# A planned attention and feed-forward block: first loads on two queues, another count of filler products, mode switches in the planner, priorities by a table

## The chip, the cores and the metric

The kernel runs on one core of a Trainium2 chip. The core has five engines that work side by side, each on its own queue of instructions: TensorE (PE in the profile; PEld are its weight loads), VectorE (DVE), ScalarE (ACT), GpSimd (POOL) and SyncE (SP), which here only issues transfers. ScalarE can issue transfers too. The metric is device microseconds of one execution; the figure for a kernel is the median of several runs.

## The reference

The input `x` has 2048 tokens of 448 values in bf16. It is normalized once, and both branches use the result:

```
xn = layernorm(x)
q, k, v = split(xn @ wqkv)               # 16 heads of 28
logits[s, w] = q[s] . k[s - 2 w] / sqrt(28)    # w = 0..7, masked where s - 2 w < 0
A = (softmax(logits) @ v[s - 2 w]) @ wo  # each token looks at 8 tokens, two apart
B = gelu(xn @ w1 + b1) @ w2 + b2         # 448 -> 1792 -> 448
out = x + A * silu(B)
```

## The kernel before

The even tokens stand in one half of the token axis and the odd ones in the other, so that "two apart" becomes "next to one another". There are 16 tiles of 128 tokens (`NT`), four chunks of 512 (`CH`), and 18 attention blocks (`BLK`) of 112 or 128 queries, each with the 128 keys before and at them.

A product of depth 448 is three products of depth 128 and a tail of depth 64. Tails of two results are put side by side in the two halves of the array (64-row mode): `batch` (L391 to L420) makes two "closed" jobs (their three full products first, then the tail) and two "opened" ones (tail first), with all tails of a batch in one task. Scores (`attn`, L541) use depth 28 and run four at a time in 32-row mode.

The stages of work, by function:

- `stats`, `rstds`, `norm`: statistics of a tile on VectorE (L341, L342), the square root on ScalarE (L351), `rstd` and the normalized tile `xn` on VectorE (L354, L369, L371). Tiles 0 to 7 are transposed by TensorE (L381) and copied to `xnT` by VectorE or ScalarE (L376 to L381); tiles 8 to 15 by a transposing DMA that SP issues.
- `qk`: query and key products of four heads each (L430, L433), in pieces of 256 tokens for the first chunk and of 512 after it. `vproj`: value products of a block (L450, L453). For these the columns of `wqkv` for queries and keys are loaded into `wraw` and spread to `wqk`, 28 columns padded to 32, by ScalarE or VectorE (L324 to L333).
- `ff1`: the first feed-forward product (L472, L475) and gelu on ScalarE with the bias `b1` (L479). `b1` is loaded as rows, transposed by TensorE (L628) and copied by VectorE (L632).
- `ff2`: the second feed-forward product (L498), bias, tanh and the gate `g` (L514, L520, L524).
- `attn`: scores, exp on ScalarE (L547), the mask on VectorE (L555), the product with the values (L562, PV below), normalization (L569, L574), then a transposing DMA into `oT`.
- `final`: the product with `wo` (L589), gate (L594), residual (L599), store (L603).

No order is written by hand. Each piece of work becomes a `_Task` with an engine (or two that could do it), a cost in us, the tasks that it depends on, buffers that it takes and gives, and a priority. `_Plan.run` (L73 to L123) lists the tasks that are ready, finds the one that could start first, and of all that could start on its engine within 0.12 us (`SLACK`) takes the one with the highest priority. `emit` then issues the instructions in the order of the planned starts; every engine carries out its queue in that order, so a wait of one instruction holds up all behind it. A task that may run on ScalarE or VectorE is put where it would end first. Priorities are numbers in the code: for the first chunk's work 95 to 99, for chunk stages `p` in `project` (L654), `100 - c` for attention (L675), `85 - c` and `60 - 4 * c` for the feed-forward products (L679, L691).

At the beginning nothing can be multiplied, so up to 40 filler products on a tile of zeros are planned on TensorE with the lowest priority, each with a cost of 0.26 us (L272 to L276). A batch of tails carries 0.12 us more in its cost for the array's change of mode (`SWITCH`, L255).

Loads (`dma`, L290) are planned as an issue on SP or ACT of 0.45 us and a transfer of so many KB at 310 KB per us, with 1.7 us until it has landed. All but the second tile of `x` are issued by SP: `x` tile 0, `wv`, `wraw` and its tail `wraw3`, `x` tiles 2 and 3, `b1`, then the rest.

Of the kernel before, what the change touches and what calls it, by code (L numbers as in the profile page):

```python
# [14 lines left out]
SLACK = 0.12  # L15
TABLE = 1.28


# [9 lines left out]
class _Task:  # L28
    __slots__ = ("eng", "cost", "deps", "fn", "prio", "take", "give", "slots",
                 "start", "end", "on", "ndep", "users", "tail", "seq", "table", "limit")  # L30


class _Plan:
# [6 lines left out]

    def add(self, eng, cost, fn, deps=(), prio=0, take=(), give=(), tail=0.0, table=(), limit=None):
# [4 lines left out]
        t.fn, t.prio, t.give, t.tail, t.table, t.limit = fn, prio, give, tail, table, limit  # L46
        t.take = {}
# [12 lines left out]

    def _at(self, t, e, free):
        at = free.get(e, 0.0)
        for p, n in t.take.items():
            if len(p.free) < n or p.fifo and p.fifo[0] is not t:
                return None
            at = max(at, sorted(p.free)[n - 1][0] + HOP)
        if t.table and self.table not in t.table:
            at += TABLE
        for d in t.deps:
            at = max(at, d.end - d.tail + 0.02 if d.on == e else d.end + HOP)  # L70
        return at

    def run(self):  # L73
# [4 lines left out]
        free = {}  # L78
        self.table = None
        ready = [t for t in self.tasks if not t.ndep]  # L80
        order = []
        while ready:
            cand = []
            for t in ready:
                ways = []
                for e, c in zip(t.eng, t.cost):
                    at = self._at(t, e, free)
                    if at is not None:
                        ways.append((at + (c if len(t.eng) > 1 else 0.0), at, e, c))
                if ways:  # L90
                    _, at, e, c = min(ways)
                    cand.append((at, t, e, c))
            if not cand:
                raise RuntimeError("the plan is stuck: " + str([(t.seq, t.eng, t.fn.__qualname__) for t in ready[:20]]))
            first = min(cand, key=lambda k: k[0])
            near = [k for k in cand if k[2] == first[2] and k[0] <= first[0] + SLACK]
            at, t, e, c = min(near, key=lambda k: (-k[1].prio, k[0], k[1].seq))
            if t.limit is not None and at > t.limit:
                t.fn, c = None, 0.0
            t.on, t.start = e, at  # L100
            if t.table and self.table not in t.table:
# [42 lines left out]
def kernel(  # L144
# [13 lines left out]
    P = 128  # L158
# [90 lines left out]
    def act(n):  # L249
        return 0.19 + n / 1200.0  # L250

    def dve(n, r=1):
        return 0.15 + n / (960.0 * r)

    SWITCH = 0.12  # L255

# [14 lines left out]
    t_warm = plan.add("DVE", 0.3, memset("vector", warm[:], 0.0), [t_on], prio=100)  # L271
    for _ in range(40):  # L272
        def fn(k):
            nc.tensor.matmul(buf(p_b, k)[:], warm[:, :P], warm[:], start=True, stop=True)  # L274
        t_warm = plan.add("PE", 0.26, fn, [t_warm], -1, take=(p_b,), limit=12.0)
        t_warm.give = ((p_b, t_warm, 0),)  # L276
# [10 lines left out]
    t_vw = [plan.add("DVE", 0.08, memset("vector", v[:, :, DH:DH + 1], 1.0), [t_on], prio=96) for v in p_v.bufs]  # L287
    t_E = [plan.add("DVE", 0.08, memset("vector", e[:, :, NQ:], 0.0), [t_on], prio=95) for e in p_E.bufs]

    def dma(eng, dst, src, kb, prio, deps=()):  # L290
        def fn(_):
            (nc.sync if eng == "SP" else nc.scalar).dma_start(dst, src)
        a = plan.add(eng, 0.45, fn, [t_on] + list(deps), prio)
        return plan.add("DMA", kb / 310.0, lambda _: None, [a], prio, tail=1.7)

# [14 lines left out]
    def ktiles(ap):  # L310
# [78 lines left out]
    def batch(close, opened, prio):  # L389
# [9 lines left out]
        def f2(k):  # L399
            todo = [[(j, i) for i, j in enumerate(every) if j.half == h] for h in range(2)]  # L400
            while todo[0] or todo[1]:
                for h in range(2):
                    if todo[h]:
# [3 lines left out]
                        else:  # L407
                            j.tail(buf(p_b, k, i - len(close)), True, False)
        tt = plan.add("PE", pairs * pe(every[0].n) + SWITCH, f2, f + [d for j in opened for d in j.deps] + [d for j in every for d in j.late],
                      prio + 0.3, take=sum(((p_b,) + j.into for j in opened), ()), give=((p_tok, f[0], 0),), tail=0.15)  # L410
        for i, j in enumerate(close):
# [54 lines left out]
    def ff1(c, mt, half, prio, gate):  # L466
# [10 lines left out]
        def evac(a, own, i):  # L477
            def fn(k):
                nc.scalar.activation(buf(p_h, own, i)[:], buf(p_b, own, i)[:], ACT.Gelu_apprx_tanh,  # L479
                                     bias=b1[:, mt:mt + 1])  # L480
            t_h[(c, mt)] = plan.add("ACT", act(CH) + 0.05, fn, [a, t_b1] + gate, prio + 3,
                                    give=((p_b, own, i),), table=("gelu",))
# [48 lines left out]
    def attn(b, prio, gate, early):  # L531
# [5 lines left out]
        def f1(k):  # L537
            for g in range(G):
                for hl in range(4):
                    r = slice(32 * hl, 32 * hl + 32)  # L540
                    nc.tensor.matmul(buf(p_b, k, hl)[:, g * nq:(g + 1) * nq], kT[g][r, k0:k0 + P],  # L541
                                     qT[g][r, q0:q0 + nq], start=True, stop=True)
        a = plan.add("PE", 0.34, f1, deps + early, prio, take=(p_b,) * 4, tail=0.15)
        pv, exps = [], []
        for hl in range(4):
# [18 lines left out]
            pv.append(plan.add("PE", 0.105, f4, [w, t_v[b]] + pv[-1:], prio + 3, take=() if hl else (p_b,),  # L564
                               give=((p_E, e, 0),) + ((v_at[b],) if hl == 3 else ()), tail=0.15))
# [5 lines left out]
        r = plan.add("DVE", 0.18, f5, [pv[-1]], prio + 4, take=(p_rd,))  # L571

# [35 lines left out]
    for t in range(TPC):  # L608
# [10 lines left out]
    t_b2 = dma("SP", b2[:], B_b2.rearrange("(o d) -> o d", o=1).to_broadcast((P, D)), 112, 81)  # L619
    t_wo = [dma("SP", wo[:, 0:3, :], ktiles(A_wo[0:KF, :]), 336, 80),  # L620
             dma("SP", wo[:64, 3, :], A_wo[KF:D, :], 56, 79)]
# [15 lines left out]
    for m, w, n, lo, hi in masks:  # L637
# [29 lines left out]
    project(0)  # L667
    t_os = [plan.add("POOL", 0.6, memset("gpsimd", o[:], 0.0), [t_xT[3]]) for o in p_os.bufs]
    t_wo.append(plan.add("POOL", 0.4, memset("gpsimd", wo[64:, 3, :], 0.0), [t_xT[3]]))
# [58 lines left out]
```

## Time and profile before

| | us |
|---|---|
| median of 6 runs | 172.37 |
| lowest and highest | 171.96, 172.57 |
| the profiled execution | 172.63 |
| its span, first to last instruction | 170.6 |
| TensorE busy in the span | 163.5 |
| VectorE, ScalarE busy | 109.4, 107.8 |

The profile is of one execution. In a row of the timeline the first number is the start in us after the first instruction, the second the length; "x4" is the number of instructions; brackets give the idle time of the engine before it and what ended that. "L472" is line 472 of the kernel. A busy TensorE is not one at its peak, as products overlap; the distance from start to start says how fast they go. In a row of windows, each engine's busy time in the stretch is followed by its number of instructions. The four digits rows of the page cut the span in 40 equal slices.

### The profile page before, as it was taken

The numbers are of one execution on the slowest core, as the hardware profiler recorded it, in microseconds if no ns is written. First come the engines' busy times: TensorE is split into PE (matmuls) and PEld (weight loads), VectorE is DVE, ScalarE is ACT, GpSimd is POOL, SyncE is SP. The second block draws the span as 40 slices with busy tenths as digits, with TensorE's granted clock in tenths as the row PEclk, the third lists the DMA queues.
The fourth block names the chain that finished last, engine by engine and source line by source line (L and its number), as shares of the span: only waits on it lengthen the run. The fifth ranks groups of instructions, "written<-read, shape, count | busy, mean of one in ns | idle before, by whom it ended". The sixth has DMA issues, their size and how long they took to land.

```text
span 170.6 us, 3510 instructions
## 1 busy us (share of the span) xinstructions
PE 163.5 (96%) x1372; PEld 78.9 (46%) x1372; DVE 109.4 (64%) x298; ACT 107.8 (63%) x197; POOL 5.0 (3%) x18
## 2 busy tenths in 40 slices
PE   7999988999999999999999999999999999999990
PEld 2455543434555544444334565434465533455540
DVE  5689887219898988896004789601689951375663
ACT  3175339968785097878889584799964599611120
POOL 7300000000000000000000000000000000000000
PEclk9999999999999999999999999999999999999999
DMA  5999980001444221211100021300012320001001
GB/s 152 253 347 270 335 295 8 0 4 30 93 99 87 54 58 27 58 29 27 27 4 0 0 61 27 81 2 4 27 26 60 81 58 0 0 27 56 27 27 54
DMA packets 21740, 12.26 MB, mean 72 GB/s; under 512 B 13724, under 2 KB 21212, under 8 KB 21724
## 3 DMA queue, kind: packets, MB, share of 16 engines
q1 hardware_dynamic: 21580, 11.93, 26.0%
q8 instruction: 10, 0.16, 0.4%
q10 hardware_dynamic: 144, 0.11, 0.2%
q14 instruction: 6, 0.05, 0.1%
HBM read 7.06 MB, written 1.84 MB: 52 GB/s over the span
## 4 chain that ended last, share of the span: by engine, by line
PE 91%; DVE 5%; ACT 1%; issue 1%; DVEq 0%; ACTq 0%
PE bank L498 25%; PE bank L472 20%; PE bank L430 12%; PE bank L589 7%; PE bank L450 6%; PE bank L562 4%; PE bank L274 4%; PE bank L475 4%; PE bank L541 3%; PE bank L433 2%; PE bank L453 1%; DVE st L341 1%; PE bank L381 1%; DVE xn L369 1%; ACT L479 1%
## 5 line engine op out<-in xcount | busy, mean ns | idle before, releaser
L498 PE MATMUL bank<-w,h 128*128 128x448 bf16 x224 | 46.4, 352 | 0.0
L547 ACT ACTIVATE E<-bank 128x448 bf16<-128x448 f32 (+1 forms) x72 | 33.7, 556 | 14.5 <-PE bank L541 14.5
L472 PE MATMUL bank<-xnT,w 128*128 128x512 bf16 x168 | 39.3, 380 | 0.0
L479 ACT ACTIVATE h<-bank,b 128x512 bf16<-128x512 f32 x56 | 34.4, 692 | 2.9 <-PE bank L475 2.8
L498 PEld LDWEIGHTS <-h 128*128 128x128 bf16 x224 | 20.9, 97 | 18.5
L472 PEld LDWEIGHTS <-w 128*128 128x128 bf16 x168 | 14.9, 97 | 20.5 <-issue 5.1
L430 PE MATMUL bank<-xnT,wqk 128*128 128x512 bf16 (+1 forms) x120 | 24.3, 337 | 0.0
L555 DVE TENSOR_TENSOR E<-E,m_gen 128x448 bf16<-128x448 bf16 x64 | 22.0, 384 | 2.1 <-ACT E L547 2.0
L520 ACT ACTIVATE t<-y 128x448 f32<-128x448 f32 x16 | 9.4, 588 | 21.1 <-DVE y L514 21.1
L562 PEld LDWEIGHTS <-E 128*128 128x128 bf16 x288 | 12.7, 96 | 9.7 <-DVE E L555 2.0
L514 DVE TENSOR_TENSOR y<-bank,b 128x448 f32<-128x448 f32 x16 | 9.8, 621 | 10.8 <-PE bank L498 10.8
L524 DVE SCALAR_TENSOR_TENSOR g<-t,y 128x448 bf16<-128x448 f32 x16 | 9.9, 619 | 9.3 <-ACT t L520 9.3
L589 PE MATMUL bank<-wo,oT 128*128 128x448 bf16 x64 | 14.5, 352 | 0.3 <-DVE y L514 0.2
L261 DVE CAST kT<-bank 128x256 bf16<-128x256 f32 (+1 forms) x9 | 4.8, 534 | 15.1 <-PE bank L430 10.6
L562 PE MATMUL bank<-v,E 128*128 128x29 bf16 x288 | 14.4, 176 | 0.0
L430 PEld LDWEIGHTS <-wqk 128*128 128x128 bf16 x120 | 10.3, 97 | 8.6 <-issue 1.9
L594 DVE SCALAR_TENSOR_TENSOR sg<-bank,g 128x448 bf16<-128x448 f32 x16 | 10.0, 622 | 4.3 <-PE bank L589 3.5
L450 PE MATMUL bank<-wv,xnT 128*128 128x448 bf16 x54 | 12.6, 353 | 0.0
L574 DVE TENSOR_TENSOR os<-bank,rd 112x448 bf16<-112x448 f32 (+1 forms) x18 | 11.2, 625 | 1.0
L341 DVE BATCH_NORM_STATS2 st<-x_sb 128x6 f32<-128x448 bf16 x16 | 9.7, 604 | 1.1 <-DMA x_sb<-in_A_x_dram 1.1
L259 ACT CAST qT<-bank 128x256 bf16<-128x256 f32 (+1 forms) x13 | 6.1, 471 | 4.4 <-PE bank L433 3.0
L274 PE MATMUL bank<-warm 128*128 128x512 bf16 x19 | 7.2, 546 | 1.3 <-DVE warm L266 1.3
(52 smaller groups left out, 122.4 us busy)
## 6 DMA issues: line engine op xcount, KB each, us to landing
out_dram<-o SPq DMA_DIRECT2D x16, 112.0 KB, 1.7
w<-in_B_w_dram SPq DMA_DIRECT2D x1, 1568.0 KB, 13.6
x_sb<-in_A_x_dram SPq DMA_DIRECT2D x3, 448.0 KB, 9.1
w<-in_B_w_dram SPq DMA_DIRECT2D x1, 1344.0 KB, 10.0
wraw<-in_A_wqkv_dram SPq DMA_DIRECT2D x1, 672.0 KB, 6.4
w<-in_B_w_dram SPq DMA_DIRECT2D x2, 224.0 KB, 8.5
x_sb<-in_A_x_dram SPq DMA_DIRECT2D x3, 112.0 KB, 4.8
wv<-in_A_wqkv_dram SPq DMA_DIRECT2D x1, 336.0 KB
```

The source lines that it names most:

```text
L274: nc.tensor.matmul(buf(p_b, k)[:], warm[:, :P], warm[:], start=True, stop=True)
L341: nc.vector.bn_stats(out=s[:], in_=x_sb[:, t, :])
L430: nc.tensor.matmul(ps[:, :n], wqk[:, kt, hs, :], xnT[:, kt, cs], start=start, stop=stop)
L450: nc.tensor.matmul(ps[:, :D], xnT[:, kt, k0:k0 + P], wv[:, kt, :], start=start, stop=stop)
L472: nc.tensor.matmul(ps[:], w1[:, kt, ms], xnT[:, kt, cs], start=start, stop=stop)
L479: nc.scalar.activation(buf(p_h, own, i)[:], buf(p_b, own, i)[:], ACT.Gelu_apprx_tanh, bias=b1[:, mt:mt + 1])
L498: nc.tensor.matmul(ps[:, :D], buf(*h_at[(c, mt)])[:, j * P:(j + 1) * P], w2[:, mt, :], start=(mt == 0), stop=(mt == NMT - 1))
L547: nc.scalar.activation(buf(p_E, k)[:, :, :nq], buf(p_b, a, hl)[:, :4 * nq].rearrange("p (g q) -> p g q", g=4), ACT.Exp, scale=SCALE)
L555: nc.vector.tensor_tensor(out=E[:, :, :nq], in0=E[:, :, :nq], in1=m[:, :, :nq], op=ALU.mult)
L562: nc.tensor.matmul(ps[:, h, :DH + 1], buf(p_E, e)[:, g, :], buf(*v_at[b])[:, h, :DH + 1], start=True, stop=True)
L574: nc.vector.tensor_tensor(out=buf(p_os, k)[:nq, :D].rearrange("p (h c) -> p h c", h=H), in0=buf(p_b, po)[:nq, :].rearrange("p (h c) -> p h ...
L589: nc.tensor.matmul(ps[:, :D], oT[:, kt, t * P:(t + 1) * P], wo[:, kt, :], start=(kt == 0), stop=(kt == KT - 1))
```

## The change

Six things change, and the new order follows from all of them together.

1. *Loads.* The third k-tile of `wv` and of `wraw`, and one half of each of their tails, are issued by ACT instead of SP. The planner counts a transfer at 340 instead of 310 KB per us. Each spread of `wraw` to `wqk` depends on its own part of the load. The later tiles of `x` come after them.
2. *Fillers.* The first ten are planned at 0.43 us, the others at 0.22.
3. *Modes.* A task has a `mode` (128, 64 or 32). A TensorE task in another mode than the one before it is planned 0.095 us later, and while the array is in a tiled mode, tiled tasks get 30 more priority.
4. *Costs.* Those of ScalarE operations, gelu, the scores, PV and the reciprocal are other numbers.
5. *Priorities* of stages come from the table `PRIO`.
6. *Memsets* of `E`, of `os` (now only its last 64 columns) and of a part of `wo` go to GpSimd at the beginning.

```diff
+SWITCH = 0.095
+TILED = 30
...
+        if e == "PE" and t.mode != self.mode:
+            at = max(at, free.get(e, 0.0) + SWITCH)
         return at
...
-            at, t, e, c = min(near, key=lambda k: (-k[1].prio, k[0], k[1].seq))
+            tiled = first[2] == "PE" and self.mode != 128
+            at, t, e, c = min(near, key=lambda k: (-k[1].prio - (TILED if tiled and k[1].mode != 128 else 0), k[0], k[1].seq))
...
     def act(n):
-        return 0.19 + n / 1200.0
+        return 0.15 + n / 1130.0
...
-    SWITCH = 0.12
...
-    for _ in range(40):
+    for i in range(40):
...
-        t_warm = plan.add("PE", 0.26, fn, [t_warm], -1, take=(p_b,), limit=12.0)
+        t_warm = plan.add("PE", 0.43 if i < 10 else 0.22, fn, [t_warm], -1, take=(p_b,), limit=12.0)
...
-    t_E = [plan.add("DVE", 0.08, memset("vector", e[:, :, NQ:], 0.0), [t_on], prio=95) for e in p_E.bufs]
+    t_os = [plan.add("POOL", 0.1, memset("gpsimd", o[:, D:], 0.0), [t_on], prio=94) for o in p_os.bufs]
+    t_wo = [plan.add("POOL", 0.45, memset("gpsimd", wo[64:, 3, :], 0.0), [t_on], prio=93)]
+    t_E = [plan.add("POOL", 0.1, memset("gpsimd", e[:, :, NQ:], 0.0), [t_on], prio=95) for e in p_E.bufs]
...
-        return plan.add("DMA", kb / 310.0, lambda _: None, [a], prio, tail=1.7)
+        return plan.add("DMA", kb / 340.0, lambda _: None, [a], prio, tail=1.7)
...
-    t_wv = [dma("SP", wv[:, 0:3, :], ktiles(A_wqkv[0:KF, 2 * D:]), 336, 98)]
-    t_wv += [dma("SP", wv[64 * i:64 * i + 64, 3, :], A_wqkv[KF:D, 2 * D:], 56, 98) for i in range(2)]
-    t_raw = dma("SP", wraw[:], ktiles(A_wqkv[0:KF, 0:2 * D]), 672, 97)
-    t_raw3 = [dma("SP", wraw3[64 * i:64 * i + 64, :], A_wqkv[KF:D, i * D:(i + 1) * D], 56, 96)
+    t_wv = [dma("SP", wv[:, 0:2, :], ktiles(A_wqkv[0:2 * P, 2 * D:]), 224, 98),
+            dma("ACT", wv[:, 2:3, :], ktiles(A_wqkv[2 * P:KF, 2 * D:]), 112, 98)]
+    t_wv += [dma(("SP", "ACT")[i], wv[64 * i:64 * i + 64, 3, :], A_wqkv[KF:D, 2 * D:], 56, 97) for i in range(2)]
+    t_raw = [dma("SP", wraw[:, 0:2, :], ktiles(A_wqkv[0:2 * P, 0:2 * D]), 448, 96)] * 2
+    t_raw += [dma("ACT", wraw[:, 2:3, :], ktiles(A_wqkv[2 * P:KF, 0:2 * D]), 224, 96)]
+    t_raw3 = [dma(("SP", "ACT")[i], wraw3[64 * i:64 * i + 64, :], A_wqkv[KF:D, i * D:(i + 1) * D], 56, 95)
               for i in range(2)]
     for t in range(2, TPC):
-        load_x(t, 1, 96, "SP")
+        load_x(t, 1, 94, "SP")
...
-        t_wqk.append(plan.add(("ACT", "DVE"), (0.94, 0.39), fn, [t_raw] + t_wz, 96))
+        t_wqk.append(plan.add(("ACT", "DVE"), (0.94, 0.39), fn, [t_raw[kt]] + t_wz, 96))
...
-        tt = plan.add("PE", pairs * pe(every[0].n) + SWITCH, f2, ...
+        tt = plan.add("PE", pairs * pe(every[0].n), f2, ...
+                      mode=64)
...
-        a = plan.add("PE", 0.34, f1, deps + early, prio, take=(p_b,) * 4, tail=0.15)
+        a = plan.add("PE", 0.15, f1, deps + early, prio, take=(p_b,) * 4, tail=0.15, mode=32)
...
+    PRIO = {"project": (88.5, 80.5, 64.5, 82.5),
+            "attn": (518, 478.5, 466, 469.5),
+            "ff1": (81, 86, 47, 55),
+            "ff2": (77, 62.5, 2.5, 29.5),
+            "final": (32.5, 106.5, 13, 13.5, 16, 30, 30, 21)}
...
-        p = (80, 79, 62, 58)[c]
+        p = PRIO["project"][c]
...
-                exps += attn(b, 100 - c, gate, gels)
+                exps += attn(b, PRIO["attn"][c], gate, gels)
...
-            p = 85 - c
+            p = PRIO["ff1"][c]
...
-                ff2(t, 60 - 4 * c)
+                ff2(t, PRIO["ff2"][c])
     for t in range(NT):
-        final(t, 62 - t if t < NT - 2 else 40)
+        final(t, PRIO["final"][t // 2])
```

More of the change, by code (lines that the diff above doesn't have):

```diff
@@ L29 @@
     __slots__ = ("eng", "cost", "deps", "fn", "prio", "take", "give", "slots",
-                 "start", "end", "on", "ndep", "users", "tail", "seq", "table", "limit")
+                 "start", "end", "on", "ndep", "users", "tail", "seq", "table", "limit", "mode")
 class _Plan:
@@ L39, in __init__, with add @@
         self.tasks = []
-    def add(self, eng, cost, fn, deps=(), prio=0, take=(), give=(), tail=0.0, table=(), limit=None):
+    def add(self, eng, cost, fn, deps=(), prio=0, take=(), give=(), tail=0.0, table=(), limit=None,
+            mode=128):
         t = _Task()
@@ L46, in add @@
         t.fn, t.prio, t.give, t.tail, t.table, t.limit = fn, prio, give, tail, table, limit
+        t.mode = mode
         t.take = {}
@@ L79, in run @@
         self.table = None
+        self.mode = 128
         ready = [t for t in self.tasks if not t.ndep]
@@ L100, in run @@
             t.on, t.start = e, at
+            if e == "PE" and t.fn is not None:
+                self.mode = t.mode
             if t.table and self.table not in t.table:
@@ L408, in f2 @@
                             j.tail(buf(p_b, k, i - len(close)), True, False)
-        tt = plan.add("PE", pairs * pe(every[0].n) + SWITCH, f2, f + [d for j in opened for d in j.deps] + [d for j in every for d in j.late],
-                      prio + 0.3, take=sum(((p_b,) + j.into for j in opened), ()), give=((p_tok, f[0], 0),), tail=0.15)
+        tt = plan.add("PE", pairs * pe(every[0].n), f2, f + [d for j in opened for d in j.deps] + [d for j in every for d in j.late],
+                      prio + 0.3, take=sum(((p_b,) + j.into for j in opened), ()), give=((p_tok, f[0], 0),), tail=0.15,
+                      mode=64)
         for i, j in enumerate(close):
@@ L480, in fn @@
                                      bias=b1[:, mt:mt + 1])
-            t_h[(c, mt)] = plan.add("ACT", act(CH) + 0.05, fn, [a, t_b1] + gate, prio + 3,
+            t_h[(c, mt)] = plan.add("ACT", 0.69, fn, [a, t_b1] + gate, prio + 3,
                                     give=((p_b, own, i),), table=("gelu",))
@@ L563, in f4 @@
                                      start=True, stop=True)
-            pv.append(plan.add("PE", 0.105, f4, [w, t_v[b]] + pv[-1:], prio + 3, take=() if hl else (p_b,),
+            pv.append(plan.add("PE", 0.12, f4, [w, t_v[b]] + pv[-1:], prio + 3, take=() if hl else (p_b,),
                                give=((p_E, e, 0),) + ((v_at[b],) if hl == 3 else ()), tail=0.15))
@@ L570, in f5 @@
                                  buf(p_b, po)[:nq, :].rearrange("p (h c) -> p h c", h=H)[:, :, DH])
-        r = plan.add("DVE", 0.18, f5, [pv[-1]], prio + 4, take=(p_rd,))
+        r = plan.add("DVE", 0.25, f5, [pv[-1]], prio + 4, take=(p_rd,))
         def f6(k):
@@ L619 @@
     t_b2 = dma("SP", b2[:], B_b2.rearrange("(o d) -> o d", o=1).to_broadcast((P, D)), 112, 81)
-    t_wo = [dma("SP", wo[:, 0:3, :], ktiles(A_wo[0:KF, :]), 336, 80),
+    t_wo += [dma("SP", wo[:, 0:3, :], ktiles(A_wo[0:KF, :]), 336, 80),
              dma("SP", wo[:64, 3, :], A_wo[KF:D, :], 56, 79)]
@@ L667 @@
     project(0)
-    t_os = [plan.add("POOL", 0.6, memset("gpsimd", o[:], 0.0), [t_xT[3]]) for o in p_os.bufs]
-    t_wo.append(plan.add("POOL", 0.4, memset("gpsimd", wo[64:, 3, :], 0.0), [t_xT[3]]))
     project(1)
```

## The prediction

> **What bounds the kernel now.** I read the page first (busy shares, slices), then the chain that ended last, then the windows of each stage, and last the two stretches of the timeline where the chain leaves TensorE.
>
> ```profile
> PE 163.5 (96%) x1372; PEld 78.9 (46%) x1372; DVE 109.4 (64%) x298; ACT 107.8 (63%) x197; POOL 5.0 (3%) x18
> PE   7999988999999999999999999999999999999990
> DMA  5999980001444221211100021300012320001001
> PE 91%; DVE 5%; ACT 1%; issue 1%; DVEq 0%; ACTq 0%
> ```
>
> TensorE is busy for 96% of the span and 91% of the chain. Its work is fixed, so only three things can move the end: when useful products begin, holes in the stream, and the price of changing the array's mode. The windows tell where holes are (columns: stretch, its length, busy time of PE, PEld, DVE, ACT, POOL, clock, DMA share, GB/s).
>
> ```profile
> 8.61:26.50 17.89, 16.60 (x130) 9.16 (x129) 15.11 (x50) 9.30 (x21) 0.00 (x0) 1.00 0.96 298
> 33.30:78.70 45.40, 45.39 (x482) 22.06 (x481) 36.27 (x95) 32.81 (x66) 0.00 (x0) 1.00 0.25 53
> 90.00:135.00 45.00, 44.70 (x479) 23.01 (x478) 29.36 (x74) 33.45 (x62) 0.00 (x0) 1.00 0.13 31
> 146.50:165.60 19.10, 19.10 (x103) 9.88 (x102) 11.51 (x21) 3.60 (x8) 0.00 (x0) 1.00 0.09 30
> ```
>
> After 26.5 us there is 0.01 + 0.30 us of idle TensorE left. So nothing after the first feed-forward stage has more than 0.3 us to give. The hole is before 26.5 us, and the timeline shows it (start, length, instruction; in brackets the idle time before it and what ended it):
>
> ```profile
> 6.35 0.15 PEld L274 LDWEIGHTS <-warm 128*128 128x128 bf16 x1 [0.28 <-issue]
> 9.40 0.94 ACT L259 COPY wqk<-wraw 128x896 bf16<-128x896 bf16 x1 [4.05 <-DMA wraw<-in_A_wqkv_dram]
> 9.45 0.74 PE L450 MATMUL bank<-wv,xnT 128*128 128x448 bf16 x3
> 10.03 0.98 PE L430 MATMUL bank<-xnT,wqk 128*128 128x256 bf16 x6
> 24.12 1.28 ACT L479 ACT_TABLE_LOAD   x1 [4.42 <-DVE b L632]
> 24.84 0.38 PE L381 MATMUL bank<-ident,xn 128*128 128x128 bf16 x4 [0.36 <-DVE xnT L261]
> 26.16 0.38 PE L381 MATMUL bank<-ident,xn 128*128 128x128 bf16 x4 [0.93 <-ACT h L479]
> ```
>
> Two things. The bias b1 reaches ScalarE only at 24.1 (its copy L632 stands behind statistics on VectorE), so the gelu table and the first gelu are late, banks stay full, and the transposes L381 stand still. From one start to the next a transpose takes 0.056 us; the group of eight at 23.88 should be followed at 24.33 and is at 24.84, the next at 25.06 and is at 26.16: 0.5 + 1.1 = **1.6 us of hole**. And the first query/key product starts at 10.03, 0.66 us after wraw landed (ACT was released at 9.40). The value products fill TensorE up to 10.03.
>
> **Mode switches and priorities.** Scores and 64-row tails put the array in another mode. From row starts, a 448-column product follows another after 0.189 us and a score group follows one after 0.285: about 0.095 us for each switch. I counted switches in the issue order of both built programs: 89 before, 89 after, with the same split by kind. So the new price and the bonus for staying in a tiled mode change the order but save 0 x 0.095 = **0 us**. Useful products are equal in number too (1353), summing to 152.6 us from the first query/key product to the end in both orders. New costs of gelu, exp and copies only change the order as well. So the priorities can win only holes: 0.3 us after 33 us. I count -0.1, with bounds -0.3 and +1.5. For the upper bound I compared ScalarE's work between the exps of successive blocks with TensorE's work between their scores. It exceeds it in three places (17.8 against 16.3, 4.5 against 4.2, 2.7 against 2.4 us), by 2.1 us in all. At the largest the next block has 2.3 us of value and 2.65 us of feed-forward products ahead of its PV products, so most of it is covered.
>
> **The b1 transpose** moves from after the query/key products to before the first value tails. Its copy on VectorE now stands after the statistics of tile 7, by my sum at about 18 us, before the first gelu. ScalarE then loads its gelu table while TensorE makes the first tiles, and tiles 4 to 7 are transposed before the stage. The 1.6 us hole goes: **-1.6**. What is late next in that stage is VectorE: from the landing of wraw to the fourth xn of the second chunk it has three weight casts (0.39, 0.39, 0.27), six statistics (0.60 + 0.18 each), six xn (0.40 + 0.20), two xnT (0.42), two q copies (0.41) and small ones, about 11.7 us, while TensorE has 9.7 us of products from its first query/key product to the stage. If wraw lands at 8.8 both end at about 21: no new hole, but no slack either. w1 landed 10.0 us after an issue at 6.86, at 16.9, and is not in the way.
>
> **The loads.** SP keeps x0, two k-tiles of wv, half of the rest, two k-tiles of wraw, half of wraw3; ACT gets x1 (as before), one k-tile of wv (112 KB), 56 KB, one k-tile of wraw (224 KB), 56 KB. That is four more issues on ACT's queue, 0.4 to 0.6 us each by SP's rows, and the fifth waits for x1 (3.24 us: a DMA semaphore is reused). ACT's first table load thus moves from 1.22 to about 3.9 and ends at 5.2; its first sqrt goes from 4.32 to 5.2. It was due at 4.3, but VectorE was busy with tile 1 until 5.0, so xn0 is about 0.4 us later. Eleven fillers at 0.427 us end at 1.26 + 4.7 = 5.96, about when xn0 is ready; before, seventeen ran to 7.57. So the transposes start a microsecond earlier and the fillers' cut is worth 1.1 us by itself, but only up to the weights.
>
> When does wraw land? In the trace 672 KB took 6.4 us from an issue at 2.98. The new SP part is issued at 2.36; by that row it lands at 2.36 + 6.4 = 8.8. The rule against this is in the Trainium skill, "DMA: Bandwidth & Descriptors", section "Issuing engines are not separate DMA queues": transfers of any issuing engine run on the same 16 DMA engines and interleave, and a second issuer saves only issue time. By the rule the SP part ends after 1400 KB instead of 1344 have passed: 9.37 + 56 KB at some 330 GB/s, about 9.5. The row for it: the DMA share from 2.5 to 4.0 us is already 1.03 at 311 GB/s. But from 4.0 to 5.5 it falls to 113 GB/s, so a microsecond of bandwidth is lost that a second stream may or may not fill. Bounds 7.6 (no dip at all) to 9.8; I take **8.8**.
>
> Now what I think matters most. ACT's order after is: sqrt, sqrt, **cast of wqk (waits for wraw), copy of xnT for tile 1**, value copies. Before, VectorE made that copy at 8.4, ahead of the weights. The second value product needs xnT of tile 1, and TensorE issues it before all query/key products. So their start is: landing 8.8, cast 0.94, copy 0.59 (as ACT's 512-wide copy of kT), tail 0.19 and switch 0.10, three products 0.57, hops 0.1: 8.8 + 2.5 = **11.3 us** against 10.03: **+1.3**. By the skill's rule it would be 12.0, +2.0. Behind that copy on ACT wait both value copies and the next sqrt; VectorE's rstd of tile 2 waits for that, with slack, since x2 lands only at about 10. The b1 load, behind wraw3 in SP's queue, is waited for by TensorE ahead of the value tails; by its place it lands 0.3 to 0.6 us after wraw, under the cast and copy (1.5 us). It would cost only if it landed later than 10.3.
>
> Memsets of E, os and a row of wo go to or forward on GpSimd: 13 small ones of 0.1 to 0.2 us, done by about 5.5; the first exp comes after 30 us. VectorE loses 0.35 us of memsets at 2.0, in a stretch where it waits for x anyway. Nothing.
>
> **Sum**, on the profiled execution (172.63 us; span 170.6, 2.0 around it): +1.3 - 1.6 - 0.1 = -0.4, a span of 170.2 and a time of 172.2. The profiled execution is 0.26 above the median of the runs, 172.37, so the forecast is **171.9**.
>
> **Rivals.**
> (a) *The dip does not return*: wraw lands at 7.6 to 8.2, the start costs 0 to +0.6, total about -1.3: 171.0. For it: 14 of 16 engines had finished wraw by 8.3, and only two held it to 9.37. Against: those are waits of single packets (1.2 us each) that two queues do not remove.
> (b) *The cast in front of the copy costs more than the hole gives*: ACT holds xnT of tile 1 until wraw has landed and been cast. At a landing of 9.8 the query/key products start at 12.3 and the feed-forward stage at 22, +2.3 - 1.6 = +0.7: 173.0, slower. It decides from a landing of about 9.5 on (+2.0 - 1.6 - 0.1 = +0.3). For it: the skill's rule above gives just that.
> (c) *New holes in the attention stages*, 1 us or more, where ScalarE's work exceeds TensorE's: 173.0. Against: before ran such stages with 0.3 us lost.
> (d) *The array goes cold*. TensorE stands still from about 8.2 to 10.4 with only a filler and small products. Granted clock reads 1.00 throughout, but the fillers' spacing (their weight loads above stand 0.43 us apart up to 6.35) went to 0.216 us only at 6.7, after 5.4 us of work. The skill, "TensorE: Matmul & The Clock Gate", Part 1, says that about 3.4 us of idleness halve the clock again. The trace had 1.6 us of hole with 0.216 us spacing after it, so the row says no cost; if it happened, 3.4 us of query/key work at half speed would cost up to 1.7: 173.6.
> (e) *The change does nothing*: start and hole cancel within 0.3.
>
> **How the numbers follow.** My sum 171.9 (own range 171.4 to 172.4): 0.40, of which 0.24 lies over 0.2% below the median (0.34 us, about what a measurement can tell), 0.14 within, 0.02 above. (a) 0.22, faster. (b) 0.20, slower. (c) 0.10 and (d) 0.06, slower. (e) alone 0.02. Faster 0.46, same 0.16, slower 0.38. The range takes in (a) to a landing of 7.6 less a little, 170.6, and (b), (c) and most of (d): 173.9.
>
> **What would show it.** First query/key product at 11.3, its wait ended by ACT's xnT copy; that copy right behind the wqk cast; b1 copied before 19 us; no idle TensorE between transposes before the first gelu; 0.2 to 0.4 us of idle TensorE after 33 us. A start before 10.5, or holes over 1 us after 33 us, would make the forecast wrong.

## The result

The changed kernel takes 170.44 us (median of 18 runs, 169.76 to 172.06), the kernel before 172.33 (37 runs beside them). The ratio is **0.9905**, with a 95% interval of 0.9884 to 0.9927: about 1.6 us faster. The forecast was 171.9, with a range of 170.6 to 173.9; applied to the 172.37 that the forecast started from, the ratio gives 170.7, at the lower end of the range. The profiled execution of the changed kernel took 171.72 us, its span is 169.1. That is 0.9 us less than the profiled execution of before, but 1.6 us less in span: 2.7 us of the changed one lie outside the span and 2.0 of the one before. (Over the 18 runs of the changed kernel the median is 1.9 outside and a span of 168.4.) So the account below is made of spans.

From the page of the changed kernel: busy times and shares of the chain.

```profile
PE 161.7 (96%) x1367; PEld 78.4 (46%) x1367; DVE 105.7 (62%) x281; ACT 112.6 (67%) x206; POOL 3.8 (2%) x26
PE 91%; DMA 5%; DVE 1%; issue 0%; ACTq 0%; DVEq 0%
```

The shares hardly differ from before; but VectorE's 5% of the chain are down to 1%, and DMA, by the load of `b1r` at the start, now has 5%. The windows of the changed kernel, with the stretch between the start and the first query/key product cut out:

```profile
8.61:11.29 2.68, 1.64 (x8) 0.68 (x9) 2.27 (x7) 2.15 (x4) 0.00 (x0) 1.00 0.88 220
11.29:26.50 15.21, 15.21 (x124) 8.69 (x123) 13.74 (x47) 11.65 (x26) 0.00 (x0) 1.00 1.00 312
33.30:78.70 45.40, 45.40 (x485) 21.82 (x484) 34.95 (x90) 35.86 (x68) 0.00 (x0) 1.00 0.25 50
90.00:135.00 45.00, 45.00 (x431) 23.01 (x430) 29.76 (x71) 31.38 (x59) 0.00 (x0) 1.00 0.15 38
```

By these rows all idle time ahead of the last product now lies before 11.29: from there TensorE is busy in the whole of each stretch. (How far such rows can be trusted is a question of its own, below.) The timeline of the changed kernel, where the forecast placed its numbers:

```profile
8.94 0.94 ACT L267 COPY wqk<-wraw 128x896 bf16<-128x896 bf16 x1 [3.18 <-DMA wraw<-in_A_wqkv_dram]
...
9.65 0.18 PE L641 MATMUL bank<-ident,b1r 14*128 14x14 bf16 x1 [1.39 <-DMA b1r<-in_B_b_dram]
...
9.78 0.58 ACT L267 COPY xnT<-bank 128x512 bf16<-128x512 bf16 x1
...
11.29 0.82 PE L443 MATMUL bank<-xnT,wqk 128*128 128x256 bf16 x6
...
17.38 0.14 DVE L645 CAST b<-bank 128x14 f32<-128x14 bf16 x1
...
20.23 1.06 PE L393 MATMUL bank<-ident,xn 128*128 128x128 bf16 x16
...
21.13 1.46 PE L485 MATMUL bank<-xnT,w 128*128 128x512 bf16 x6
...
21.97 1.28 ACT L492 ACT_TABLE_LOAD   x1
23.27 2.42 ACT L492 ACTIVATE h<-bank,b 128x512 bf16<-128x512 f32 x4
```

ScalarE casts at 8.94, copies xnT of tile 1 behind that, and the first query/key product starts at 11.29 (10.03 before). The sixteen transposes of tiles 4 to 7 stand in one row ahead of the feed-forward stage, without a bracket (before, they stood within it from 23.88 to 26.5, with two waits), and the first gelu runs at 23.27 instead of 25.42.

Three starts make the account, in us of the profiled executions:

| | before | changed | difference |
|---|---|---|---|
| first query/key product | 10.03 | 11.29 | +1.26 |
| from it to the last product | 155.95 | 152.97 | -2.98 |
| last product to the end of the span | 4.67 | 4.80 | +0.13 |
| span | 170.64 | 169.06 | -1.58 |

By the forecast's sum the useful products between add up to 152.6 us at their own spacing. So before lost 3.3 us after its first query/key product and the changed kernel loses 0.4. Where the difference of 2.98 lies can be read from start to start, each distance less the usual one between two such products:

| place in before | us |
|---|---|
| two waits between transposes, from 24.27 and from 25.01 | 0.52 + 1.09 |
| second query/key product, waits for a cast of `wqk` (from 10.15) | 0.13 |
| b1 transpose with its change of mode (19.23); in the changed kernel it stands ahead of the first query/key product | 0.2 |
| two tails one behind the other instead of side by side (26.47) | 0.22 |
| later: from 68.44, 122.31, 132.11 and 132.35 | 0.17 + 0.36 + 0.12 + 0.24 |

That is 3.1 us. The changed kernel has no such hole; 0.1 comes back in smaller delays. After 33 us it is 0.9. Two of the later holes stand in the chain of before:

```profile
122.02 0.64 DVE y L514
...
122.70 0.92 PE bank L589 x4
...
132.02 0.54 ACT E L547
...
132.61 0.92 PE bank L589 x4
```

The chain leaves TensorE for VectorE's y and for ScalarE's E, and comes back to the products with `wo`. In the changed kernel neither step is there: its second feed-forward products begin at 34.1 instead of 41.0 and its `wo` products at 64.9 instead of 54.5, so other work stands at that place. That the new order removes these waits is read from the two traces; which of the new priorities does it was not tried apart.

### The profile page after: what moved, and what is told of

Read it like the earlier page. It is cut to its first block, busy times and chain, and to the rows that moved or that the text cites. A ratio compares the mean times of both kernels' runs of the same rounds, so it can differ in the third digit from the quotient of the medians.

```text
span 169.1 us, 3502 instructions
## 1 busy us (share of the span) xinstructions
PE 161.7 (96%) x1367; PEld 78.4 (46%) x1367; DVE 105.7 (62%) x281; ACT 112.6 (67%) x206; POOL 3.8 (2%) x26
## 4 chain that ended last, share of the span: by engine, by line
PE 91%; DMA 5%; DVE 1%; issue 0%; ACTq 0%; DVEq 0%
PE bank L511 25%; PE bank L485 22%; PE bank L443 13%; PE bank L602 7%; PE bank L463 6%; PE bank L575 5%; PE bank L488 4%; PE bank L554 3%; DMA b1r<-in_B_b_dram 3%; PE bank L446 3%; DMA wv<-in_A_wqkv_dram 2%; PE bank L466 2%; PE bank L393 1%; DVE sg L607 1%; DVE o L612 0%
## 5 line engine op out<-in xcount | busy, mean ns | idle before, releaser
L568 DVE TENSOR_TENSOR E<-E,m_gen 128x448 bf16<-128x448 bf16 x64 | 22.9, 386 | 2.5 <-ACT E L560 1.9
L267 ACT CAST qT<-bank 128x512 bf16<-128x512 f32 (+1 forms) x15 | 7.5, 501 | 4.7 <-PE bank L446 3.7
L269 DVE CAST kT<-bank 128x512 bf16<-128x512 f32 (+1 forms) x6 | 3.9, 645 | 10.8 <-PE bank L443 10.6
L267 ACT CAST v<-bank 128x448 bf16<-128x448 f32 x14 | 7.4, 535 | 4.6 <-PE bank L466 2.6
```

The costliest lines, as they stand in the source:

```text
L267: nc.scalar.copy(o, i)
L568: nc.vector.tensor_tensor(out=E[:, :, :nq], in0=E[:, :, :nq], in1=m[:, :, :nq], op=ALU.mult)
```

## The experiments

Times are medians; ratios are against the kernel before, run on the same chip, with 95% intervals. "Release" is the start of ScalarE's wqk cast, that is, the landing of SP's part of wraw. In most runs tasks were moved in the finished plan, by

```diff
     plan.run()
+    def move(t, *behind):
+        plan.order.remove(t)
+        plan.order.insert(max(plan.order.index(b) for b in behind) + 1, t)
```

**The bias copied early, in the kernel before** (only the 0.14 us copy of b1 moves, right behind its transpose).

```diff
+    move(t_b1, t_b1T)
```

> The kernel before with one instruction moved: the copy of b1 on VectorE (L632) stands right behind its transpose instead of behind the statistics of tiles 8 to 10. Theory (the late bias is the cause of the hole before 26.5 us): the gelu table is loaded at about 19.7 instead of 24.1, the transposes of tiles 4 to 7 find free banks, the hole of 1.6 us goes and nothing else moves: 170.8, first query/key product still at 10.0. Rival (the hole is a shortage of banks or of VectorE that only moving the transposes ahead of the stage removes): under 0.5 us gained.

171.37 us, ratio 0.9958 [0.9935, 0.9981]; 170.8 was expected. The timeline of this run:

```profile
19.52 0.17 DVE L633 CAST b<-bank 128x14 f32<-128x14 bf16 x1 [0.37 <-PE bank L628]
...
24.93 0.61 PE L381 MATMUL bank<-ident,xn 128*128 128x128 bf16 x8 [0.36 <-DVE xnT L261]
```

b1 is there at 19.7 and the first gelu runs at 21.24. Of the two holes between transposes, the one of 1.09 us is gone; the one of 0.52 stays, and it waits for VectorE's copy of the tile before, as the bracket says. The stretch from the first query/key product to the last is 155.00 us, 0.95 less. So the late bias was 1.1 of the 1.6 us and not all of it.

**The bias copied late, in the changed kernel.** b1 is copied to a spare tile (`b1x`) as now, and from there to b1 only behind the statistics of tile 10.

```diff
-        nc.vector.tensor_copy(b1[:], buf(p_b, a)[:].bitcast(BF16)[:, :NMT])
+        nc.vector.tensor_copy(b1x[:], buf(p_b, a)[:].bitcast(BF16)[:, :NMT])
...
+    st10 = t_st[10].fn
+    def late(k):
+        st10(k)
+        nc.vector.tensor_copy(b1[:], b1x[:])
+    t_st[10].fn = late
```

> The changed kernel with b1 held back: VectorE copies it to a spare tile at 17.4 as now, and from there to its place only behind the statistics of tile 10, at about 24, as in the kernel before; the order of all else is the changed one. Theory (the late bias costs only because transposes stand in the feed-forward stage and wait for its banks; here they stand ahead of it): gelu starts 2 us later, eight banks and the two feed-forward products behind the stage cover it, 0 to +0.3 us. Rival (a late bias costs 1.6 us wherever the transposes stand): +1.6, 172.2.

170.87 us, ratio 0.9933 [0.9910, 0.9957]. Its timeline:

```profile
20.80 1.46 PE L486 MATMUL bank<-xnT,w 128*128 128x512 bf16 x6
...
23.39 0.14 DVE L719 COPY b<-b1x 128x14 f32<-128x14 f32 x1
...
23.61 1.28 ACT L493 ACT_TABLE_LOAD   x1 [1.99 <-DVE b L719]
24.90 2.42 ACT L493 ACTIVATE h<-bank,b 128x512 bf16<-128x512 f32 x4
```

The gelu comes 4.1 us after the stage's first product (2.1 in the changed kernel), the table load waits for b1 as it did before, and TensorE shows no hole: 152.94 us from first query/key to last product against 152.97. The median is 0.4 us above the changed kernel's, which these intervals don't tell apart. With the transposes ahead of the stage, the late bias costs TensorE nothing. In this order it is their place that counts, and the early bias is not needed for it. (The opposite run, the kernel before with only its transposes moved ahead of the stage, was not made.)

**The xnT copy on VectorE** (tile 1's copy goes back to VectorE, ahead of the weights).

```diff
+    t_xT[1].on = "DVE"
+    move(t_xT[1], t_xT[0], t_xT[1].deps[0])
```

> The changed kernel with one instruction moved: the xnT copy of tile 1 from ScalarE, where it stands behind the cast of wqk, to VectorE, right behind the copy of tile 0. Theory: the value tails then wait only for b1r, which landed at 9.61, so the first query/key product comes at about 10.85 instead of 11.29: -0.45 us. Rival (the cast in front of the copy did not set the start, the weights did): 0.

170.05 us, ratio 0.9901 [0.9864, 0.9939]. Release 8.40, first query/key product 10.22: 1.82 behind it, against 2.35 in the changed kernel. The copy behind the cast costs **0.5 us**, and all of that reaches the last product (0.5 earlier for the same release). The medians and their intervals can't tell this from the changed kernel.

**The b1 transpose behind the value tails** (and the copy left on ScalarE).

```diff
+    move(t_b1T, tails[1])
```

> The changed kernel with only the transpose of b1 on TensorE moved behind the tails of the first query/key batch; the xnT copy of tile 1 stays on ScalarE behind the cast. Theory: the copy ends at 10.36 and the wait for b1r (9.61) is hidden under it: 0, the first query/key product stays at 11.2 to 11.3. Rival (the load of b1 is what holds the start, as the chain of the changed kernel names it): start at about 10.5, -0.7 us.

170.63 us, ratio 0.9927 [0.9893, 0.9962]. Release 8.18, start 10.53: 2.35 behind it again. The chain of the changed kernel had named another holder for this stretch:

```profile
4.44 5.17 DMA b1r<-in_B_b_dram
...
9.83 0.32 PE bank L282
10.15 0.62 PE bank L466 x2
```

It follows the b1 load because that ended last ahead of the products there. With the transpose gone from that place nothing is earlier: the xnT copy behind the cast, ending a little later, held the same products.

**Both moved.**

> As the run with the copy on VectorE, and TensorE transposes b1 behind the tails of the first query/key batch instead of ahead of the value tails. Theory: value products are done by 9.0, the start is set by wraw and its casts (8.91 + 0.39, the second cast 9.9): first query/key product at 9.5 to 9.9, -1.4 us there; VectorE's chain to the fourth xn of the second chunk ended at 20.5 and gives back only its waits, so 0.4 to 0.8 us of hole come before the stage: -0.6 to -1.0 in all, about 169.6. Rival (VectorE's chain sets the first feed-forward stage): no gain over the run with the copy alone.

170.45 us, ratio 0.9925 [0.9898, 0.9952]: no gain over the changed kernel in the medians, where 0.6 to 1.0 was expected. The start is only 0.46 behind the release (8.91, 9.37), 1.9 less than in the changed kernel. The last product is at 163.55. With the changed kernel's distance, release + 155.3, it would be at 164.2: of the 1.9 us **0.7** reach the last product. The stretch from first to last grew by 1.2 to 154.18, and three places account for most of it. Two are waits, in the timeline

```profile
9.91 0.72 PE L446 MATMUL bank<-xnT,wqk 128*128 128x256 bf16 x5 [0.26 <-ACT wqk L267]
...
11.82 0.45 PE L393 MATMUL bank<-ident,xn 128*128 128x128 bf16 x4 [0.44 <-DVE xn L381]
```

From start to start, the second query/key product is 0.43 us late, behind ScalarE's cast, and the first transpose after it 0.6, behind VectorE's xn. The third is the b1 transpose, which now stands in this stretch (about 0.1). The feed-forward stage does not wait: VectorE's fourth xn of the second chunk ends 10.9 us behind the release (19.82), and the row of transposes ahead of the stage has no hole. So VectorE is next in line, but at 11.8 and not at the stage, where the forecast had it.

**One queue.** The same plan and order, but ScalarE's four loads of weights are issued by SP.

```diff
-            (nc.sync if eng == "SP" else nc.scalar).dma_start(dst, src)
+            (nc.sync if eng == "SP" or kb != 112 or prio != 99 else nc.scalar).dma_start(dst, src)
```

> The changed kernel in its own planned order with the four loads that ACT issues (k-tiles of wv and wraw, halves of the tails) issued by SP instead. If a second queue gains nothing (all run on the same 16 engines): wraw lands as now at 8.9, within 0.2, and ScalarE's table load comes back to 1.2 us: 0. If it fills the dip in the transfer rate: wraw lands at 9.3 to 9.5, the start 0.4 to 0.6 later: +0.5 us.

170.04 us, ratio 0.9893 [0.9845, 0.9940]: nothing is lost. SP's part landed at 7.7 and the last k-tile at 8.5; the start is 2.65 behind the release instead of 2.35, since here the rows of b1, behind the weights in the one queue, came at 9.0 and held the value tails. The releases of the profiled runs lie like this (us):

| | release |
|---|---|
| wraw on two queues | 7.55, 8.07, 8.18, 8.40, 8.61, 8.80, 8.84, 8.85, 8.91, 8.94 |
| on SP alone | 7.70, 7.95, 9.40, 9.48 |

The means are 8.5 and 8.6. They are not of quite the same thing: on two queues, and at 7.70, the release is the landing of two k-tiles (448 KB); at 7.95, 9.40 and 9.48 it is that of all three (672 KB). A gain by the second queue cannot be told from this scatter.

**More fillers**: seven products in the place of the eleventh filler, so seventeen ahead of the first transpose, as before.

```diff
+            for _ in range(7 if i == 10 else 1):
                 nc.tensor.matmul(buf(p_b, k)[:], warm[:, :P], warm[:], start=True, stop=True)
```

> The changed kernel with 17 fillers instead of 11 ahead of the first transpose. Theory (the weights and the copy behind the cast set the start, not the fillers): the transposes come 1.3 us later, the first query/key product stays at 11.3: 0. Rival (the cut of fillers is part of the gain): +1 us.

170.07 us, ratio 0.9888 [0.9832, 0.9944]. The first transpose is 0.5 us later (6.75) and not 1.3, as the fillers went over to their quick pace at 5.0 us here; the first query/key product is 2.35 behind its release (7.55) as ever. In this order the cut in fillers is worth nothing.

**No fillers**: the filler tasks stay in the plan and issue nothing; the result does not depend on them.

> The changed kernel with no fillers at all. If the array is cold until it has worked some microseconds: value products at 0.37 us instead of 0.19 and query/key products of 256 columns at 0.21 instead of 0.11 for 3 us or more, the first one at about 11.9, and the stage ends 1.5 to 2.5 us later: +1.5 to +2.5 us. If fillers are not needed: 0.

172.44 us, ratio 1.0030 [0.9994, 1.0067]: all of the gain is lost. The clock's row of the page and the timeline of this run:

```profile
PEclk9999999999999999999999999999999999999999
...
7.59 1.30 PE L463 MATMUL bank<-wv,xnT 128*128 128x448 bf16 x3
...
11.91 1.46 PE L443 MATMUL bank<-xnT,wqk 128*128 128x256 bf16 x6
...
14.18 1.04 PE L443 MATMUL bank<-xnT,wqk 128*128 128x256 bf16 x8
```

Three value products take 1.30 us instead of 0.74 as in the changed kernel, six query/key products 1.46 instead of 0.82; at 14.18 eight take 1.04, the usual pace. In this execution it cost 1.34 us at the last product, by the medians 2.0.

**The planner alone**: mode switches, costs and stage priorities of the change; loads, fillers and memsets of before.

> The planner's part of the change alone: modes, costs and priorities as changed; loads, fillers and memsets as before. In its order VectorE copies xnT of tile 1 ahead of the casts, b1 is late again and three transposes stand in the feed-forward stage. Theory: start at 10.0, the hole of about 1.6 us still there, the 0.8 us of small holes after 33 us gone: 171.6. Rival (the planner's numbers carry the gain): 170.5 or less.

173.81 us, ratio **1.0117** [1.0096, 1.0137]: slower. Three transposes are in the feed-forward stage again, b1 is copied at 24.06, and new holes appear in the attention, in its timeline

```profile
54.80 0.20 PE L550 MATMUL bank<-qT,kT 32*128 32x112 bf16 x1 [0.29 <-ACT E L556]
55.23 0.20 PE L550 MATMUL bank<-qT,kT 32*128 32x112 bf16 x1 [0.23 <-ACT E L556]
55.86 0.37 PE L550 MATMUL bank<-qT,kT 32*128 32x112 bf16 x14 [0.42 <-DVE os L583]
```

with two score products one by one behind ScalarE's exps and the next behind VectorE's `os`: 1.4 us from start to start. Its last product is where that of before was (165.76), and the work of VectorE and the store behind it take 5.7 us instead of 4.7. The profiled span is 0.8 us over that of before; the medians say 2.0. The spans of its other three runs, 172.1 to 172.2, are longer than the profiled one (171.5), and the median span of before beside them was 170.05, so the 2.0 is in the span too; where in it the trace at hand can't show. The gain that was expected of this half is not there.

**The loads alone**: loads, fillers and memsets of the change, the planner of before.

> The loads, fillers and memsets of the change alone; the planner, its costs and priorities as before. In its order the xnT copy of tile 1 stands behind the cast on ScalarE, b1 is early and the four transposes stand late in the first feed-forward stage. Theory: start at 11.3 (+1.3), first hole gone (-1.6), small holes after 33 us as before: about -0.3, 172.0. Rival (two queues carry the gain): 170.7.

172.79 us, ratio 1.0047 [1.0014, 1.0080]: slower too. Release 8.84, start 11.19, the same 2.35 and +1.2; and in the timeline the transposes wait as before:

```profile
25.68 0.38 PE L385 MATMUL bank<-ident,xn 128*128 128x128 bf16 x4 [0.63 <-ACT h L483]
...
26.26 0.61 PE L385 MATMUL bank<-ident,xn 128*128 128x128 bf16 x8 [0.19 <-ACT h L483]
```

The waits from start to start are 0.8 and 0.36 us, and the later holes of before are all there (0.17, 0.36, 0.13 and 0.24).

So each half costs (+1.2% and +0.5%) and both together gain 1%: neither half carries the gain. Of the three orders only the one made with both halves has the transposes ahead of the stage and no later hole. Finer parts (the mode price, the costs, the table of priorities) were not run apart.

**Transposes behind the first feed-forward tiles.** If VectorE's run to the fourth xn were what the stage waits for, the products of the first four feed-forward tiles, which need only chunk 0, can run while it makes the xn of tiles 4 to 7. The copy and the b1 transpose are moved as above. `firsts[-1]` is the last full product of these four tiles; behind it go the transposes of tiles 4 to 7, then their copies, all on VectorE, then the statistics of tiles 8 to 10:

```diff
+    last = firsts[-1]
+    for t in range(4, 8):
+        tr, up = t_xT[t].deps[0], t_xT[t]
+        up.on = "DVE"
+        move(tr, last)
+        last = tr
+    for t in range(4, 8):
+        move(t_xT[t], last)
+        last = t_xT[t]
+    for t in range(8, 11):
+        move(t_st[t], last)
+        last = t_st[t]
```

> The changed kernel with three moves: the xnT copy of tile 1 on VectorE ahead of the casts, b1 transposed behind the first query/key tails, and the transposes of tiles 4 to 7 (their copies all on VectorE) behind the first four tiles of the feed-forward stage instead of ahead of it. Theory: the start follows the landing of wraw by 0.5 us instead of 2.35, and the stage no longer waits for VectorE's chain of 11.5 us from that landing, so at the same landing the last product comes 1.0 to 1.8 us earlier than in the changed kernel: about 169.2, if the last part of w1 (19.4 in the changed kernel's trace) does not hold the tails. Rival (transposes in the stage bring the hole of the kernel before back): no gain over the changed kernel.

**169.89 us, ratio 0.9855** [0.9827, 0.9882]; the changed kernel, run beside it, follows below. The timeline of this run:

```profile
8.07 0.94 ACT L267 COPY wqk<-wraw 128x896 bf16<-128x896 bf16 x1 [2.30 <-DMA wraw<-in_A_wqkv_dram]
...
9.29 0.82 PE L448 MATMUL bank<-xnT,wqk 128*128 128x256 bf16 x6
...
11.03 0.45 PE L393 MATMUL bank<-ident,xn 128*128 128x128 bf16 x4 [0.17 <-DVE xn L381]
...
18.74 1.46 PE L490 MATMUL bank<-xnT,w 128*128 128x512 bf16 x5
...
21.97 1.06 PE L393 MATMUL bank<-ident,xn 128*128 128x128 bf16 x16
```

The stage starts 10.7 us behind the release, 0.3 us before VectorE's fourth xn is done, and the sixteen transposes stand in one row without a wait, inside the stage. So transposes in the stage need not bring the hole back: here b1 is early and VectorE makes its copies in time. The first query/key product is 1.2 behind the release and not 0.5, since the value products fill TensorE up to 9.29. The last product is at 162.77; by the changed kernel's release + 155.3 it would be at 163.4. So 0.6 us are won at equal release, less than the 1.0 to 1.8 that were expected: the start is 1.1 earlier for its release, and the stretch from first to last product, 153.48, is 0.5 longer, by a wait of 0.33 from start to start at 11.03 (VectorE's xn again) and the b1 transpose. The run with the first two moves alone had won 0.7. The transposes' new place therefore shows no gain of its own in the traces; what the lower ratio owes to it is open.

**The changed kernel again.**

> The changed kernel once more, beside the run with three moves. Theory (in its order the first query/key product follows the landing of wraw by 2.35 us and the rest takes 153.0 us): whatever the landing is in this execution, the first query/key product is 2.35 us behind it and the last product 155.3 us behind it; the time is 170.4 within 0.5.

170.77 us, ratio 0.9906 [0.9881, 0.9932]; release 8.80, start 11.15, last product 164.12: 2.35 and 155.3 behind the release, as expected. The version above is 0.5% below it, and the two intervals only touch.

## Why the prediction was right or wrong

The direction was right, at a stated chance of 0.46 for faster against 0.38 for slower. The change was forecast at -0.5 us and measured at -1.6 to -1.9. Most of what is missing is in one step. The two large terms, a later start and the hole of the first stage, nearly cancel, as the forecast had them; that the kernel is clearly faster comes from what it had at nothing or nearly so. The clear gain is therefore in part luck.

- *Start of the query/key products, +1.3 to 11.3*: right, 11.29. All six executions on two queues that kept the copy on ScalarE and the fillers have it 2.35 behind the release; the sum gave 2.5. Of these 2.35, the copy behind the cast is 0.5 and, by the run with both moved, the b1 transpose is what holds once the copy is away. The profiled execution has a late release, though: 8.94, against a mean of 8.5 over the two-queue runs. With that mean the start costs +0.8. (With the loads and fillers of before the start did not follow the release: 10.0 at releases of 7.95 and 9.40, the value products filling TensorE up to then.)
- *Landing of wraw at 8.8*: within the scatter. The estimate of 9.5, worked out from the rule of the Trainium skill ("DMA: Bandwidth & Descriptors", "Issuing engines are not separate DMA queues"), was later than any landing on two queues; the rule itself, that a second issuer saves no more than issue time, agrees with the run on one queue, 0.9893 against 0.9905. Rival (a), an earlier landing, happens in single executions, with one queue (7.70) as with two (7.55).
- *First-stage hole, -1.6 by an early b1*: the size was right, the cause only in part. The bias was 1.1 of it; 0.5 was VectorE's xnT copies. In the changed kernel both are gone with the transposes ahead of the stage, and in that order an early b1 is worth nothing (152.94 with a late one).
- *Later holes, -0.1, bounds -0.3 and +1.5*: **this is the step that failed.** They were -0.9 after 33 us, in four holes; another 0.35 in two small places before 26.7 and 0.2 for the b1 transpose had no term at all. I had read 0.01 + 0.30 us of idle time from the windows. But a product's bar in the profile is 0.352 us long, while products follow one another after 0.189: a hole of up to 0.16 us is covered by the bar of the product before it, and a longer one is shown short by as much. From start to start the same stretches have 0.89. The sum of 152.6 us, which I had made, against 155.95 showed 3.3 us and not 1.9: the missing 1.4 stood in my own numbers. My bound on the side of a gain came from the same row and was too tight.
- *Switches 0, fillers' cut 0, memsets 0*: 89 switches in both, and more fillers cost nothing; the memsets were not tried apart. That the cut by itself was worth 1.1 us ahead of the weights did not hold: the fillers of before ran to 7.57 since they went over to their quick pace only at 6.7 in that execution. In the run with the early bias they did so at 4.1, and with the same seventeen fillers the first transpose is at 6.26. And nothing as against *fewer* fillers is not nothing as against none, which cost 1.3 to 2.0 us.
- *VectorE 11.7 us from the landing to the fourth xn, no new hole and no slack*: right, 11.6 (20.53), with 0.4 us to spare before its transposes at 20.9. With an earlier start it is not this chain but an earlier xn, at 11 to 12 us, that TensorE waits for.
- *Rivals.* (b) did not come, as no landing on two queues reached 9.5. (c) new holes in the attention: not here, but in the planner alone, where scores wait for exps. It was no empty fear; the same priorities on another start give it. (d) a cold array: not with the fillers. The longest stand was 8.26 to 9.65, and query/key products followed one another after 0.109 us. The skill's "TensorE: Matmul & The Clock Gate", Part 1, puts the limit at some 3.4 us of idleness, which no run here reached after warming.

Sum with what was measured, in the profiled executions: +1.26 for the start, -1.6 and -0.9 for the holes, -0.35 and -0.2 for the small places and the b1 transpose, +0.2 for the end and smaller delays: -1.6 of span. At the mean release it would be about -2.0; the runs show -1.6 by the ratio and -1.9 by the medians.

## What to carry to other kernels

Measure holes in a pipelined engine from start to start, and set the sum of all products at their own spacing against the stretch that they took: the busy share hides just the small holes that a better order removes. Where a planner makes the order, an edit is judged by the whole order that comes out, and undoing it by halves may show each half as a loss. The release that the profile names is the last of several; before counting a gain for removing it, look how much later it was than the next. Where a landing scatters, compare single traces at equal distance from it and not by their ends.

## What the runs showed of the hardware

- The load of wraw (448 or 672 KB) landed between 7.55 and 9.48 us in the profiled executions, on one queue or two; its 448 KB part alone between 7.55 and 8.94. In the changed order the first query/key product comes 2.35 us and the last product 155.3 or 155.4 us behind it, at releases from 7.55 to 8.94, so this scatter goes straight to the time.
- Without fillers, products run at about half pace from the first value product at 7.6 until about 13.0 (0.35 to 0.37 us from one value product to the next instead of 0.189, 0.213 for a query/key product instead of 0.109), while the row of the granted clock reads full speed all the time. The clock's row can't tell this state; the distance from start to start can.
- The fillers, the first at 1.25 us, went from 0.427 to 0.216 us apart at 4.1 us in one execution (the kernel before with the early bias) and at 6.7 in another (the kernel before), 2.9 and 5.5 us after the first one, though TensorE's instructions up to there are the same.
- Four more issues on ScalarE's queue moved its first table load from 1.22 to 3.98 us and its first square root from 4.32 to 5.27. With these issues on SP (the run on one queue) they are at 1.24 and 4.18, the first transpose at 5.41 instead of 6.25, and the query/key products start no earlier behind the release (2.65).
